# Attention with a gated MLP: V ahead of the third score tile at a unit's start, maxima transposed ahead of V, and 576 instead of 560 early score tiles that begin sooner

## The chip, the cores and the metric

The kernel runs on one core of a Trainium2 chip. The time is what the device takes for one execution, in microseconds (us), from start to end, with all loads from and stores to the chip's memory in it. "Before" is the kernel as it was, "after" the same kernel with the change below.

A core has five engines that run their own instruction streams and wait for one another by semaphores: TensorE (PE in the profile, its weight loads PEld), VectorE (DVE), ScalarE (ACT), GpSimd (POOL) and SyncE (SP). In this kernel SP only issues transfers, in the order of its queue.

## The reference

x has 2048 rows of 512. There are 32 heads of 16, and an MLP of width 1376 whose output gates the attention's.

```python
xn  = layernorm(x)
qkv = xn @ wqkv                                  # q, k, v: 32 heads x 2048 x 16
p   = softmax(q @ k.T * 16 ** -0.5)              # per head, 2048 x 2048
s   = (p @ v, heads joined) @ wo
g   = silu(gelu(xn @ w1 + b1) @ w2 + b2)
out = x + s * g
```

Everything is float32. The kernel splits most operands into a high and a low part and adds three products (`mm3`), and it keeps q and k as such pairs.

## The kernel before, in words

**Stages.** The first stage (to about 53 us) normalizes x, transposes it (`turn`), makes the q and k products of the first two head groups chunk by chunk (`q_first`), and four of the sixteen V products (`v_tile`). `evac` writes q and k, high and low, to scratch memory (`qk_h`, `qk_l`), from where they are loaded in the layout of attention: `load_k` for the keys of a group of four heads, `load_qs` for the queries of a *unit*. A unit is one group of heads times one chunk of 512 queries; there are 32 units.

The second stage (to about 480 us) is the written-out list `plan`: the other twelve V products (`quad`, entries "first"), the MLP's two products ("half" and "down") and the q and k products of the other groups. All its matmuls use half of the array's rows, two at a time, one on each half; `run` issues one for each half per *place*, counted in `prog["n"]`, 1488 places in all. After given places `run` calls hooks: splits and loads of weights, and `errand`, which takes one entry from the list `errands` (loads of K and Q for later units).

The third stage is attention, a loop of 512 steps (and one to drain): each step makes four transposed score tiles of 128 keys by 512 queries, one per head ("T", `t_one`), whose exponentials ScalarE writes (L656), and the V products of the step before ("V", `pv_step`, L723, a group of four heads, eight matmuls in the trace). From step 492 on the output products are woven in.

**The maxima.** The exponential needs each row's maximum before the T tiles of its unit start, so each score is made twice: once as an "S" tile of 128 queries by 512 keys (`s_one`, L174), whose maximum VectorE takes (L176), and later as a T tile. There are 2048 S tiles, 64 for each unit. An S tile uses one row half as well; `s_one` gets the half as its argument. 4 x `LEAD` = 560 of them are *early* tiles: `fill` puts them between the matmuls of the second stage, evenly from place `FILL0` on. The others go into the attention loop: `due(n)` says how many should exist at step n, and `ORDER` gives the order of a step's operations by the number of S tiles wanted. With three it is `STTTSTSV`, with four `STTSTSVTS`.

When a unit's S tiles are done, `s_end0` reduces the maxima and asks for the queries of the unit after the next. Some ticks later `flush` calls `s_end1` and `s_end2`: the maxima are transposed on TensorE (L200), copied out and written to memory (`mh_d`), from where `load_mh` brings them into the rows of QT that T multiplies.

**Banks.** S tiles take the accumulator banks of `s_ring` in turn. In attention that is twice the pool `ps_s`, which has two banks, and then the one of `ps_v` and `ps_x` that V does not use in this unit: V's sums for unit u are in `pv_pool(u)`, and at a unit's end ScalarE copies them out (`os`, L730). The transpose of the maxima takes a bank of the same ring.

**The code around the change.** In the attention loop, `tick` counts a waiting transpose down, and `flush` issues it, after a V group:

```python
            elif op == "V":
                if n:
                    pv_step(*divmod(n - 1, 16))
                for _ in range(4):
                    tick()
                flush()
```

Of the kernel before, what the change touches and what calls it, by code (L numbers as in the profile page):

```python
# [17 lines left out]
S = 2048  # L18
# [5 lines left out]
CH = 512  # L24
NCH = S // CH
# [4 lines left out]
EPS = 1e-5  # L30
SCALE = DH ** -0.5
VW = DH + 1
LEAD = 140
NW = 10
EARLY = 4
DONE = 492
FILL0 = 84
HB = 4
W2B = 2
ORDER = {0: "TTTTV", 1: "TTTTSV", 2: "TTTSTSV", 3: "STTTSTSV", 4: "STTSTSVTS"}  # L40
# [6 lines left out]
def fused(ctx: ExitStack, tc: tile.TileContext, x, wqk, wv, wo, w1, b1, w2, b2, out):  # L47
# [36 lines left out]
    NU = NG * NCH  # L84
# [14 lines left out]
    def load_k(g, pieces=range(6), eng=nc.sync, c0=0, n=S):  # L99
        both = kws[g % KB]  # L100
        for i in pieces:
            a, b = divmod(i, 3)
            r, cs = slice(64 * a + DH * b, 64 * a + DH * b + DH), slice(c0, c0 + n)
            src = rows((qk_h, qk_h, qk_l)[b], g, 1, a, c0, n)
            if both is not None:
                eng.dma_start(both[r, :, cs].bitcast(F32), src)
            else:
                for p in range(2):
                    eng.dma_start(kts[g % KB][p][r, cs].bitcast(F32), src[:, p])
# [23 lines left out]
    def load_qs(u, sides=range(2)):  # L133
        if u < NU:
            QS[u] = qzs[u % 2] if u < LEAD // 16 else qss[0][:, u % 2]
            q_rows(QS[u], u, sides)

    def ask_qs(u):
        for a in range(2):
            errands.append((load_qs, u, (a,)))  # L140
# [18 lines left out]
    def flush():  # L159
        while later and later[0][0] <= 0:  # L160
            u = later.pop(0)[1]
            s_end1(u)
            s_end2(u)

    def s_one(a):
        u, st, p = halves[a][made[a]]
        made[a] += 1
        g = u // NCH
        qi, ki = divmod(st, NCH)
        if u not in MX:  # L170
            MX[u] = qring.tile([P, GH, NCH, NCH], F32, name="mx")
        ps = s_tile()
        r, q = slice(64 * a, 64 * a + 3 * DH), QS[u]
        nc.tensor.matmul(ps, q[r, p, qi * P:(qi + 1) * P],  # L174
                         kts[g % KB][p][r, ki * CH:(ki + 1) * CH], start=True, stop=True)
        nc.vector.tensor_reduce(MX[u][:, 2 * p + a, qi, ki:ki + 1], ps, axis=AX.X, op=OP.max)  # L176
        if min(made) == 32 * (ended[0] + 1):
            v = ended[0]
            ended[0] += 1
            s_end0(v)  # L180
            later.append([12 if "seen" in prog else 8, v])
# [61 lines left out]
    for j in range(len(pairs)):  # L243
        for h in range(2):
# [4 lines left out]
            due = next((i for i in range(j, len(pairs)) if is_m[i]), len(pairs))  # L249
            nxt = next((i for i in range(j + h, len(pairs)) if is_m[i]), len(pairs))  # L250
            left = 2 * (nxt - j) + 1 - h
            need = 4 * sum(is_m[:nxt]) - 4 - nd
            room = 2 * (due + 1 - j) - h
            n = 2 if nd < len(parts) and parts[nd][2] and ready - nd > room else 1
            n = max(n, need - 2 * (left - 1))
# [27 lines left out]
    def w2_load(i):  # L283
        if i < len(ms):
            W2[ms[i][1:]] = w_new(w2[ms[i][2]], 2, "raw2")

    def w2_split(i):
        if i < len(ms):
            W2[ms[i][1:]] = w_split(W2[ms[i][1:]], "w2", W2B)
# [31 lines left out]
    with ExitStack() as s1:  # L321
# [54 lines left out]
        def v_tile(t):  # L376
            pv = a_tile((P, D))
            c, ts = t // NCH, slice(t % NCH * P, t % NCH * P + P)
            for k in range(KT):
                mm3(pv, (xh[c][:, k, ts], xl[c][:, k, ts]), (wv_h[:, k], wv_l[:, k]), k == 0, k == KT - 1)  # L380
            v_out(t, pv)

        def q_first(c):
            pq = {}
            for g in range(2):
                ps = pq["q", g, c] = a_tile((P, CH))
                for k in range(KT):
                    ks = slice(k * P, (k + 1) * P)
                    mm3(ps, (W1[g][0][:, ks], W1[g][1][:, ks]), (xh[c][:, k], xl[c][:, k]), k == 0, k == KT - 1)
            evac(list(pq), pq)  # L390
# [58 lines left out]
        for c in range(1, NCH):  # L449
            for t in range(NCH * c, NCH * c + NCH):  # L450
                turn(t)
            if c < NCH - 1:
                ln(NCH * c + NCH, NCH)
            else:
                nc.scalar.activation(warm[:, 1:], warm[:, :1], AF.Gelu_apprx_tanh)
                w1_load(0)
                w2_load(0)
                w2_load(1)
            v_tile(c - 1)
            q_first(c)  # L460
        v_tile(NCH - 1)

    keep_r = ctx.enter_context(tc.tile_pool(name="keep_r", bufs=1, side="right"))
    qring = ctx.enter_context(tc.tile_pool(name="qring", bufs=2, side="right"))
# [5 lines left out]
    qzp = qz.enter_context(tc.tile_pool(name="qzp", bufs=1, side="right"))  # L470
    for i in range(2):
        qzs.append(qzp.tile([P, 2, CH], F32R, name=f"qz{i}"))

    SYNC = mybir.DependencyInfo(mybir.DependencyClass.Sync, mybir.DependencyReason.DATA)
    prog.update(n=0, pe=0, seen=0)
# [141 lines left out]
    def quad(n):  # L617
        us = first[n]
        for u, b in zip(us, BANKS[n]):
            pool, name = {"x": (ps_x, "ps"), "m": (ps_m, "ps"), "v": (ps_v, "pv"), "t": (ps_t, "pst")}[b]  # L620
            PH[u] = pool.tile([P, CH], F32, name=name)
        for i in range(4):
            hooks = {6: [mark]} if i in (1, 2) else {}
            if n == VQ - 2 and i in (0, 2):
                hooks[3] = [lambda: w1_split(0) if i == 0 else w1_load(1)]
            run((terms(us[i], 0, i < 2), terms(us[(i + 2) % 4], 1, i < 2)), hooks)
            if i >= 2:
                for u in (us[i - 2], us[i]):
                    v_out(u[1] * NCH + u[2], PH.pop(u))
# [25 lines left out]
                         QT[u][r, p, :], start=True, stop=True)  # L655
        nc.scalar.activation(PT[u, k][:, 2 * p + a, :], ps, AF.Exp, scale=SCALE)  # L656

    load_k(0)
    load_qs(0)
    k_ones(kts[0])  # L660
    for n, e in enumerate(plan):
        if e[0] == "half":
            half(*e[1:])
        elif e[0] == "first":
            quad(e[1])
        else:
            if e[1] == parts[-2]:
                nc.scalar.activation(mhw, ident_r[:1, :1].bitcast(F32), AF.Exp)
            if e[1] == parts[-1]:
                for i in range(EARLY):  # L670
                    t_one(0, 0, i // 2, i % 2)
            down(*e[1])
        if e == ("first", VQ - 1):
            w2_split(0)
            w2_load(2)
            ask_qs(1)
            ask_k(1)
        if e[0] == "half" and pairs[e[1]][0] == ("q", NG - 1, 0) and e[2] == 1:
            kts.append([slot(p, (P, S), F32R) for p in range(2)])
            kws.append(None)  # L680
            qss.append(slot(2, (P, 2, 2, CH), F32R))
            ask_k(2)
        if n == len(plan) - 8:
            load_qt(0)
            load_mh(0)
# [151 lines left out]
    L = 16 * NU  # L837

    def due(n):
        return min(4 * L, 4 * LEAD + max(0, (4 * (L - LEAD) * n - 300) // (DONE - 1)))  # L840

    for u in range(NU):
        g, c = divmod(u, NCH)
        if c == 0 and g == KB:
            at(57, load_k, g, range(6), nc.gpsimd, 0, S // 2, pos=0)
            at(64, load_k, g, range(6), nc.gpsimd, S // 2, S // 2, pos=0)
        elif c == 0 and g > KB:
            for i in range(6):
                at(64 * (g - KB + 1) + 6 + i, load_k, g, (i,), nc.gpsimd, pos=0)
        if u >= 2:  # L850
            at(16 * u - 14, load_qt, u)
            need = min(n for n in range(L) if due(n) >= 64 * (u + 1)) + (4 if u < NU - 1 else 2)
            at(max(16 * u - 14, need), load_mh, u)
        if u < NU - 1:
            at(16 * u + 17, o_move, u, pos=0)
            at(16 * u + (25 if g < NG - 1 else 19), o_den, u, pos=0)
            at(16 * u + (31 if g < NG - 1 else 22), o_div, u, nc.gpsimd)
    T3 = range(NT - NCH, NT)
    last, late = 1, range(NW, NT)
    for t in range(NW):  # L860
        n = DONE + 2 * t
# [6 lines left out]
    for i, t in enumerate(late):  # L868
        n = L - 2 * len(late) - 1 + 2 * i
# [7 lines left out]
    for n in range(L + 1):  # L877
        ua, ka = divmod(n, 16)
        want = due(n) - sum(made)
        i = 0  # L880
        if n > 1 and (n - 1) % 16 == 0:
            s_ring[:] = [ps_s, ps_s, pv_pool((n - 1) // 16 + 1)]
            s_turn[0] = 0
        for op in ORDER[want] if n > 1 else ("TTTTV", "TTTVTSS")[n]:
            if op == "S":
                h = 1 - last if made[1 - last] - made[last] < 4 and made[1 - last] < 2 * L else last
                s_one(h)
                last = h
            elif op == "V":
                if n:  # L890
                    pv_step(*divmod(n - 1, 16))
                for _ in range(4):
                    tick()
                flush()
            else:
                if EARLY <= 4 * n + i < 4 * L:
                    t_one(ua, ka, i // 2, i % 2)
                    last = i % 2
                for f, args in todo.get((n, i), []):
                    f(*args)  # L900
                i += 1
# [56 lines left out]
```

## Time and profile before

| | |
|---|---|
| median of 3 runs | 1639.98 us (1639.7 to 1640.26) |
| the profiled execution | 1640.26 us, its span 1638.5 us |
| granted TensorE clock | 0.999 |
| PE busy | 1627.3 us (99%), 11656 matmuls |
| VectorE busy | 1389.8 us (85%) |
| ScalarE busy | 1271.9 us (78%) |
| GpSimd busy | 373.5 us (23%) |
| transfers | 116.83 MB, mean 71 GB/s |

The span goes from the first to the last instruction. Busy time is the time in which an engine had an instruction under way; matmuls overlap, so a busy PE is not PE at its peak. In a row of the timeline the first figure is the start in us from the span's start, the second the time it took (of merged rows, all of them), then engine, line, operation, what it writes and reads by the program's names, and the count; a bracket gives the idle time before it and what ended that. In a row of stretches the figures are: length, busy time (and instructions) of PE, PEld, DVE, ACT and POOL, then the granted clock, the mean busy share of the DMA engines and GB/s. In a row of waits: the engine and line that waited, for what, us in total, times, and for some the longest.

### The profile page before, as it was taken

Reading aid. Unit: us, or ns where it says so; the run is one execution under the profiler, and the core shown is the slowest. Engines: PE = TensorE matmul, PEld = TensorE weight load, DVE = VectorE, ACT = ScalarE, POOL = GpSimd, SP = SyncE. Lnnn points to the kernel's source line nnn. Section 1 sums busy time; section 2 is a strip of 40 time slices with the busy share of each in tenths; the row PEclk is TensorE's granted clock in tenths of the full one; section 3 lists DMA queues with packets and bytes.
Section 4 is the critical chain, followed back from the end, with each engine's and each line's share of the span. In section 5 each row is a group of like instructions: output and inputs, shape, how many; then the busy total and the mean of one; then the engine's idle time right before and its main releaser. Section 6 shows DMA issues by size and latency. Waiting matters only on the chain.

```text
span 1638.5 us, 31026 instructions
## 1 busy us (share of the span) xinstructions
PE 1627.3 (99%) x11656; PEld 898.3 (55%) x11656; DVE 1389.8 (85%) x2299; ACT 1271.9 (78%) x2523; POOL 373.5 (23%) x366
## 2 busy tenths in 40 slices
PE   9999999999999999999999999999999999999998
PEld 7898999988974434333334443433334443434445
DVE  7299999999988888888888888888888888888733
ACT  4333433434349999999999999999999999999984
POOL 4235565756630011001000100100100000000144
PEclk9999999999999999999999999999999999999999
DMA  6625334453330122112301411411141111110152
GB/s 200 147 72 150 113 118 130 138 135 121 111 117 26 29 50 47 31 45 49 61 26 28 79 29 28 66 31 31 36 59 32 28 28 37 32 28 22 56 191 94
DMA packets 76214, 116.83 MB, mean 71 GB/s; under 512 B 24964, under 2 KB 26244, under 8 KB 74696
## 3 DMA queue, kind: packets, MB, share of 16 engines
q1 hardware_dynamic: 72604, 102.42, 22.3%
q0 software_dynamic: 3264, 12.35, 4.5%
q8 instruction: 92, 1.51, 0.4%
q14 instruction: 58, 0.48, 0.1%
q10 hardware_dynamic: 196, 0.07, 0.0%
HBM read 84.35 MB, written 25.97 MB: 67 GB/s over the span
## 4 chain that ended last, share of the span: by engine, by line
PE 94%; DVE 2%; issue 2%; ACT 1%; POOL 1%; DMA 0%; SPq 0%; ACTq 0%; DVEq 0%; POOLq 0%
PE ps L174 23%; PE pv L723 15%; PE ps L723 15%; PE ps L506 12%; PE pst L654 12%; PE pst L506 7%; PE pv L174 3%; PE ps L77 2%; PE pv L506 2%; ACT slot L656 1%; PE pst L77 1%; POOL ol L791 1%; DVE mx L176 0%; PE ps L654 0%; POOL gx L824 0%
## 5 line engine op out<-in xcount | busy, mean ns | idle before, releaser
L176 DVE TENSOR_REDUCE mx<-ps 128x1 f32<-128x512 f32 x1808 | 1168.6, 685 | 160.3 <-PE ps L654 76.6
L656 ACT ACTIVATE slot<-pst 128x512 f32<-128x512 f32 x1533 | 806.9, 608 | 5.0 <-PE ps L174 4.5
L656 ACT ACTIVATE slot<-ps 128x512 f32<-128x512 f32 x515 | 308.7, 600 | 44.4 <-PE ps L654 9.8
L174 PE MATMUL ps<-kt,slot 48*128 48x512 f32 x864 | 327.9, 443 | 0.0
L174 PEld LDWEIGHTS ps<-kt,slot 48*128 48x128 f32 x864 | 158.2, 184 | 256.8 <-DVE mx L176 235.6
L654 PE MATMUL pst<-qt,kt 50*128 50x512 f32 x1149 | 294.1, 409 | 0.4 <-DVE gt L587 0.3
L723 PE MATMUL pv<-slot,vsb 128*32 128x512 f32 x2048 | 272.7, 605 | 0.0
L723 PE MATMUL ps<-slot,vsb 128*32 128x512 f32 x2048 | 272.5, 604 | 0.0
L506 PE MATMUL ps<-slot,w1h 64*128 64x512 f32 x1088 | 225.2, 394 | 0.4 <-ACT junk L519 0.4
L174 PE MATMUL ps<-kt,qz 48*128 48x512 f32 x512 | 211.1, 416 | 0.2
L654 PE MATMUL ps<-qt,kt 50*128 50x512 f32 x387 | 189.8, 492 | 0.0
L176 DVE TENSOR_REDUCE mx<-pv 128x1 f32<-128x512 f32 x240 | 163.8, 683 | 11.6 <-PE ps L654 7.8
L174 PE MATMUL ps<-slot,slot 48*128 48x512 f32 x432 | 166.2, 441 | 0.2
L506 PEld LDWEIGHTS ps<-slot,w1h 64*128 64x128 f32 x1088 | 153.8, 185 | 9.5 <-ACT junk L519 2.3
L654 PEld LDWEIGHTS pst<-qt,kt 50*128 50x128 f32 x1149 | 144.5, 186 | 21.5 <-issue 8.4
L506 PE MATMUL ps<-slot,w1l 64*128 64x512 f32 x544 | 154.0, 393 | 0.0
L174 PEld LDWEIGHTS ps<-slot,slot 48*128 48x128 f32 x432 | 78.6, 184 | 115.0 <-DVE mx L176 104.8
L307 POOL TENSOR_TENSOR hl<-hg,hh 128x512 fp32r<-128x512 f32 x76 | 96.9, 1297 | 129.2 <-ACT hh L306 80.8
L189 POOL TENSOR_TENSOR nmh<-nm,nmh 128x16 fp32r<-128x16 f32 x32 | 7.1, 221 | 497.9 <-DVE nm L188 266.5
L519 ACT ACTIVATE junk<-ident_r 1x1 f32<-1x1 f32 x91 | 17.8, 196 | 120.4 <-PE pst L506 104.0
L174 PEld LDWEIGHTS ps<-kt,qz 48*128 48x128 f32 x512 | 93.7, 183 | 11.8 <-DVE mx L176 2.7
L654 PE MATMUL pst<-qt,slot 50*128 50x512 f32 x384 | 97.7, 406 | 0.0
(161 smaller groups left out, 1980.7 us busy)
## 6 DMA issues: line engine op xcount, KB each, us to landing
raw<-in_w SPq DMA_DIRECT2D x88, 256.0 KB
qk_h<-hh SPq DMA_DIRECT2D x32, 256.0 KB
qk_l<-hl SPq DMA_DIRECT2D x32, 256.0 KB
qt<-qk_h SPq DMA_DIRECT2D x128, 64.0 KB
slot<-qk_h SPq DMA_DIRECT2D x96, 64.0 KB
xt<-in_x SPq DMA_DIRECT2D x16, 256.0 KB
g_d<-gt POOLq DMA_DIRECT2D x16, 256.0 KB, 3.7
qt<-qk_l SPq DMA_DIRECT2D x64, 64.0 KB
```

The costliest lines, as they stand in the source:

```text
L77: nc.tensor.matmul(ps, lhs[a], rhs[b], start=first and n == 0, stop=last and n == 2)
L174: nc.tensor.matmul(ps, q[r, p, qi * P:(qi + 1) * P], kts[g % KB][p][r, ki * CH:(ki + 1) * CH], start=True, stop=True)
L176: nc.vector.tensor_reduce(MX[u][:, 2 * p + a, qi, ki:ki + 1], ps, axis=AX.X, op=OP.max)
L189: nc.gpsimd.tensor_sub(NM[u][:, 1], nm, NM[u][:, 0].bitcast(F32))
L307: nc.gpsimd.tensor_sub(hl, raw, hh.bitcast(F32))
L506: i = nc.tensor.matmul(ps, lhs[r], rhs[r], start=first, stop=last).ins
L519: i = nc.scalar.activation(junk[:, :1], ident_r[:1, :1].bitcast(F32), AF.Copy).ins
L654: nc.tensor.matmul(ps, kts[g % KB][p][r, k * P:(k + 1) * P], QT[u][r, p, :], start=True, stop=True)
L656: nc.scalar.activation(PT[u, k][:, 2 * p + a, :], ps, AF.Exp, scale=SCALE)
L723: nc.tensor.matmul(PV[u][32 * j:32 * j + 32, :], vsb[:, k, h:h + 32], PT[u, k][:, j, :], start=(k == 0), stop=(k == NT - 1))
L791: lo.tensor_sub(ol[:, :n], src, oh[:, :n].bitcast(F32))
```

## The change

It does these things:

- `LEAD` is 144 instead of 140, so there are 576 early S tiles, and `due(n)` gives exactly three S tiles for each step from the second to step 491. Before, 1488 tiles were spread over the same steps, so that some had four.
- `FILL0` is 10 instead of 84: the early tiles begin at the start of the twelve V products. For that, the pools that hold K and Q are opened after the last transposes; three quarters of the first K and the first Q are loaded from there, ahead of the third V product and the last q and k products, and the last quarter of K after them. Unit 0 goes through its S tiles by chunks of keys first. Unit 1's queries are asked for after the first `quad` instead of after the third.
- In a unit's first step of attention the order `STTTSTSV` becomes `STTTSTVS`.
- `flush` comes before the V group instead of after it; a waiting transpose is still issued after the same number of ticks, and so lies ahead of the next step's V group instead of behind this step's.
- `load_mh` of the last unit moves by one step relative to the step in which its tiles are complete.

```diff
-LEAD = 140
+LEAD = 144
...
-FILL0 = 84
+FILL0 = 10
...
-        qi, ki = divmod(st, NCH)
+        qi, ki = divmod(st, NCH) if u else divmod(st, NCH)[::-1]
...
                 w2_load(1)
+                break
             v_tile(c - 1)
             q_first(c)
-        v_tile(NCH - 1)
...
+    load_k(0, c0=0, n=S - CH)
+    load_qs(0)
+    v_tile(NCH - 2)
+    q_first(NCH - 1)
+    v_tile(NCH - 1)
+    load_k(0, c0=S - CH, n=CH)
...
-    load_k(0)
-    load_qs(0)
     k_ones(kts[0])
...
             quad(e[1])
+            if e[1] == 0:
+                ask_qs(1)
...
         if e == ("first", VQ - 1):
             w2_split(0)
             w2_load(2)
-            ask_qs(1)
             ask_k(1)
...
     def due(n):
-        return min(4 * L, 4 * LEAD + max(0, (4 * (L - LEAD) * n - 300) // (DONE - 1)))
+        return min(4 * L, 4 * LEAD + max(0, 3 * n - 1))
...
-            need = min(n for n in range(L) if due(n) >= 64 * (u + 1)) + (4 if u < NU - 1 else 2)
+            need = min(n for n in range(L) if due(n) >= 64 * (u + 1)) + (4 if u < NU - 1 else 3)
...
-        for op in ORDER[want] if n > 1 else ("TTTTV", "TTTVTSS")[n]:
+        order = ORDER[want] if n > 1 else ("TTTTV", "TTTVTSS")[n]
+        if n > 1 and (n - 1) % 16 == 0 and order.endswith("SV"):
+            order = order[:-2] + "VS"
+        for op in order:
...
             elif op == "V":
+                flush()
                 if n:
                     pv_step(*divmod(n - 1, 16))
                 for _ in range(4):
                     tick()
-                flush()
```

## Prediction

> **What bounds the kernel now.** I read the page first: busy shares and the chain that ended last.
>
> ```profile
> PE 1627.3 (99%) x11656; PEld 898.3 (55%) x11656; DVE 1389.8 (85%) x2299; ACT 1271.9 (78%) x2523; POOL 373.5 (23%) x366
> ...
> PE 94%; DVE 2%; issue 2%; ACT 1%; POOL 1%; DMA 0%; SPq 0%; ACTq 0%; DVEq 0%; POOLq 0%
> ...
> L174 PEld LDWEIGHTS ps<-kt,qz 48*128 48x128 f32 x512 | 93.7, 183 | 11.8 <-DVE mx L176 2.7
> ```
>
> TensorE (PE) carries 94% of the chain. A busy PE can still be waiting, so next come the engines by stretches: one of the projections (first row) and the body of attention (second).
>
> ```profile
> 264.00:312.00 48.00, 48.00 (x396) 43.03 (x392) 44.21 (x69) 19.41 (x44) 31.93 (x28) 1.00 0.43 125
> ...
> 600.00:1520.00 920.00, 919.90 (x6402) 367.94 (x6396) 820.25 (x1373) 886.83 (x1725) 67.52 (x97) 1.00 0.19 39
> ```
>
> The busy figures stand in the order PE, weight loads, VectorE, ScalarE, GpSimd. In the projections VectorE (44.21 of 48 us) is at 92%, almost as tight as PE. In attention PE is full and ScalarE (886.83 of 920) close behind. What a change is worth there is read from the spacing of the V groups, so the third view is PE's timeline. A step runs from one V group (L723) to the next.
>
> ```profile
> 772.77 1.07 PE L723 MATMUL pv<-slot,vsb 128*32 128x512 f32 x8
> 773.76 0.25 PE L200 MATMUL ps<-ident_r,nmh 128*32 128x128 f32 x1
> 773.94 0.50 PE L174 MATMUL ps<-kt,slot 48*128 48x512 f32 x1
> ...
> 775.07 1.06 PE L723 MATMUL pv<-slot,vsb 128*32 128x512 f32 x8
> ...
> 794.12 1.06 PE L723 MATMUL pv<-slot,vsb 128*32 128x512 f32 x8
> ...
> 796.60 1.06 PE L723 MATMUL ps<-slot,vsb 128*32 128x512 f32 x8
> ...
> 798.72 1.07 PE L723 MATMUL ps<-slot,vsb 128*32 128x512 f32 x8
> 799.71 0.50 PE L174 MATMUL ps<-kt,slot 48*128 48x512 f32 x1
> ...
> 800.85 1.06 PE L723 MATMUL ps<-slot,vsb 128*32 128x512 f32 x8
> ...
> 807.22 1.07 PE L723 MATMUL ps<-slot,vsb 128*32 128x512 f32 x8
> ...
> 809.11 1.06 PE L723 MATMUL ps<-slot,vsb 128*32 128x512 f32 x8
> ...
> 810.10 0.72 PE L174 MATMUL ps<-kt,slot 48*128 48x512 f32 x2
> ...
> 811.41 0.50 PE L174 MATMUL ps<-kt,slot 48*128 48x512 f32 x1
> 811.84 1.06 PE L723 MATMUL ps<-slot,vsb 128*32 128x512 f32 x8
> ```
>
> Four kinds of step show. A plain one takes 2.13 us (798.72 to 800.85): 0.99 for V, then 1.14 for four T and three S tiles, which run two at a time on the two row halves. A step with a transpose of maxima (L200) takes 2.30. A unit's first step takes 2.48. A step of four S tiles and the next take 1.89 + 2.73 = 4.62, which is 0.37 over two plain ones (4.25).
>
> **The change, part by part.** *One S tile too many.* Before, 1488 score tiles are spread over 491 steps, so 15 steps carry a fourth; after, 1472 tiles make exactly three each. Saved: 15 x 0.37 = 5.6 us. Their 16 tiles move into the projections, where PE is also full: 24 products take 2.75 us there, 0.115 each.
>
> ```profile
> 67.31 2.75 PE pst L506 x24
> ```
>
> That costs 16 x 0.115 = 1.8 us. In exchange the early tiles thin out, from 560 over 1386 places to 576 over 1460 (2.4% less work for VectorE per place). The group of weight loads on the page's last row above waited 11.8 us in all, 2.7 of them for VectorE, so the gain lies between 0 and 2.7; I take 1.0.
>
> *First V ahead of the third S.* The 2.48 has its cause in two rows: ScalarE copies the old unit's sums out (os), and the third S needs that bank.
>
> ```profile
> 795.50 0.63 ACT L730 ACTIVATE os<-pv 128x512 f32<-128x512 f32 x1
> ```
>
> ```profile
> 796.18 0.18 PEld L174 LDWEIGHTS pv<-kt,slot 48*128 48x128 f32 x1 [0.31 <-ACT os L730]
> ```
>
> ```profile
> PEld pv L174 <- ACT os L730: 4.2, 14, 0.3
> PEld ps L174 <- ACT os L730: 4.2, 14, 0.3
> ```
>
> 28 of 30 boundaries show that wait. With V first it goes, and V's bank has long been free. But what is late next? The third S now opens the next step, and that step's own third S uses the same bank, three turns of the ring later. The four-S steps already have this order (`STTSTSVTS`): the S behind V starts at 810.10, VectorE reads it from 810.66, and the S that needs its bank starts only at 811.41, 1.31 later, with V 0.43 behind it.
>
> ```profile
> 810.66 1.29 DVE L176 TENSOR_REDUCE mx<-ps 128x1 f32<-128x512 f32 x2
> ```
>
> So I price a boundary as that pair: 1.89 + 2.73 = 4.62 against 2.48 + 2.12 = 4.60, or +0.02 each, +0.6 over 30. The 1.89 holds if the second S lies on the other row half than the fourth T; following the code's choice of halves step by step, it does at every boundary after the change. Ends: no wait for the bank (1.89 + 2.13) -0.58 each, -17; a fourth slot after all, +0.23 each, +7.
>
> *Maxima ahead of V.* The transpose now comes behind a step's third S and takes the ring's next bank, which is that of the step's first S: free 1.31 after that S started, where V would have started 1.14 after it. That is 0.17 of wait, and then V follows the transpose by up to 0.18 (773.76 to 773.94). Price 0.17 to 0.35, against 0.17 now (2.30 - 2.13). What queues behind the waiting transpose is the V group and with it everything on PE. Count:
>
> ```profile
> L208 DVE COPY mh<-ps x24: 268/274/279, 500.9 to 1555.7; 32x128 f32<-32x128 f32 x24
> ```
>
> 24 x (0 to 0.18) = 0 to 4.3; I take 0.1 each, +2.4. Nothing below zero, since the bank is always that one.
>
> *The early start.* The first S moves from place 87 to place 13 of the V products, which begin at 53.31 with 0.229 a place: it is due at 56.1. What it needs is K (six loads) and Q (six).
>
> ```profile
> 53.31 0.49 PE L506 MATMUL pst<-kt,slot 64*128 64x512 f32 x1
> ...
> 73.10 0.39 PE L174 MATMUL ps<-kt,qz 48*128 48x512 f32 x1
> ```
>
> ```profile
> 44.50 1.89 SPq L221 DMA_DIRECT2D raw<-in_w  x4
> ...
> 55.04 0.79 SPq L106 DMA_DIRECT2D kt<-qk_h  x2
> ...
> 65.58 0.30 SPq L131 DMA_DIRECT2D qz<-qk_h  x1
> ```
>
> ```profile
> 48.00:50.00 2.00, 2.00 (x11) 1.59 (x10) 0.00 (x0) 0.51 (x1) 0.00 (x0) 1.00 0.99 331
> 50.00:52.00 2.00, 2.00 (x10) 1.65 (x9) 0.00 (x0) 1.29 (x3) 0.04 (x1) 1.00 0.08 28
> ...
> 60.00:62.00 2.00, 2.00 (x20) 1.63 (x20) 0.00 (x0) 0.34 (x2) 0.00 (x0) 1.00 1.15 180
> ```
>
> On SP's queue the loads now follow the four weight loads of 44.50, so K can be asked for at 46.4 instead of 55.04; but the DMA engines work off those weights until 50. K's three quarters are 6 x 192 KB, Q's first half 0.2 MB: 1.38 MB at 180 GB/s (60:62, when K moved) is 7.7 us, plus about 2 to land: 59.5 to 60. Stall about 3.5 us. Ends: at the 331 GB/s of 48:50 hardly any; as long as before (55.04 to past 65.58) over 4. I take 3.4. All of PE waits behind that one S. The last K quarter is needed only at place 135, far behind its load.
>
> *Q of unit 2.* Unit 2 starts at place 337 instead of 404, but its Q is asked for by errands, one per half product. Moving unit 1's two errands up lets unit 2's run two turns earlier, at places 309 and 339; its second half is used at 340. Before, the errand of place 339 was the last K load. It went out at 147.46, and PE's S nearest place 340 started at 146.60.
>
> ```profile
> 146.60 0.39 PE L174 MATMUL ps<-kt,qz 48*128 48x512 f32 x1
> ```
>
> ```profile
> 147.46 0.43 SPq L106 DMA_DIRECT2D kt<-qk_l  x1
> ```
>
> ```profile
> SPq L755 <- DMA den_d<-dr: 78.0, 32, 10.2
> ```
>
> 0.86 late, two more issues of 0.43, and 78.0/32 = 2.4 for a small DMA to land: 4.1 us of PE waiting. Ends: 0, if SP runs ahead of PE there, and 4.5.
>
> *The clock.* Once in this trace PE falls idle that long, at its end:
>
> ```profile
> 1632.00:1635.00 3.00, 0.61 (x6) 0.41 (x4) 3.00 (x7) 0.00 (x0) 0.62 (x1) 0.93 0.47 175
> ```
>
> ```profile
> L420 PE MATMUL pv<-ident 128*128 128x128 f32 x23 | 5.2, 426 | 1.4 <-POOL ident masks.py:199 1.4
> ```
>
> ```profile
> L420 PE MATMUL pv<-ident 128*128 128x128 f32 x23 | 2.9, 285 | 0.0
> ```
>
> 0.93 means half clock from 2.6 us into that stretch, 2 us after PE's last work; two stalls of 3.4 and 4.1 should trip it too. The other two rows (0 to 6.4 us and 6.4 to 9) are the start: the same 23 transposes took 5.2 us and then 2.9, so about 5 us ran at half speed, 2.5 lost. Per stall 0 to 2.5; I take 2.0, together 4.0. The Trainium skill, "TensorE: Matmul & The Clock Gate", Part 1 (the HAM clock gate), says the gate is free-running: it halves the clock after an idle window of about 3.4 us and restores it after a busy one. The end of this trace agrees that idling halves it, though after only 2 us. By the page a stall would cost an estimated 1.7, and the sum would be 0.6 lower.
>
> Sum: -5.6 + 1.8 - 1.0 + 0.6 + 2.4 + 3.4 + 4.1 + 4.0 = +9.7 us. The profiled execution took 1640.26 (span 1638.5), 0.28 over the median of 1639.98; on the median that is 1649.7.
>
> **The rivals.** *The loads are in time.* K and Q land by 56 and SP issues unit 2's Q ahead of PE. Then 11.5 us fall away: 1638.2, not slower. It decides at a landing before 56.1 and an issue more than 3.3 us ahead of place 340. For it: 331 GB/s was reached just before. Against: K moved at 180, and unit 2's errand stands directly in front of its use. *One stall only*, with its clock: about 1643.9. *Both stalls without the clock loss*: 1645.7; for it, that no row shows a stall inside the run. *The boundary wait does not come*, its S finding its bank free: 17 to 18 less, 1631.6 with both stalls; against it the 1.31 above. *A fourth slot at each boundary*: +7, 1656.7.
>
> **How the numbers follow.** Forecast 0.45; no clock loss 0.17; one stall 0.15; loads in time 0.12; no boundary wait 0.06; fourth slot 0.05. About 0.2% (3.3 us) is what a measurement can tell from no change. Faster than that: the boundary case and the better part of the loads in time (its VectorE gain at 2.7, its transposes free), 0.09. Within: the rest of that and the small end of one stall, 0.13. Slower: 0.78. The range runs from 1638.0, which takes in half of the case without stalls, to 1654.5, where both stalls and the transposes stand at their upper ends; left out are the fourth slot, the free boundary and the other half, 0.17.
>
> **What would show it.** Right: first S between 59 and 61 with PE idle before it; a second idle stretch of about 4 us near 155, ended by a DMA of qz; PE's clock below 1.00 behind each; boundary pairs of 1.9 and 2.7; transpose steps of 2.3 to 2.5; no step of four S. Wrong: PE busy throughout 53 to 480, or boundary pairs summing to 4.1 or 4.8.

## The result, and the profile after

The changed kernel took **1656.74 us** (median of 4 runs, 1655.24 to 1657.85) against 1639.99 before, a ratio of 1.0102 with a 95% interval of 1.0084 to 1.0119: 16.75 us slower. The forecast was 1649.7. Its direction was right, its size was not, and the result lies 2.2 us above its range. The profiled execution took 1657.85 us, its span is 1656.1; between the two profiled spans lie 17.6 us.

The page of the changed kernel: engines, the chain that ended last, and the group of early score tiles (`qz`; the last two figures of a group are the idle time before it and what ended that).

```profile
PE 1631.1 (98%) x11656; PEld 903.3 (55%) x11656; DVE 1390.0 (84%) x2299; ACT 1268.7 (77%) x2525; POOL 372.1 (22%) x366
...
PE 95%; DMA 2%; DVE 2%; issue 0%; ACT 0%; POOL 0%; SPq 0%; DVEq 0%; ACTq 0%; POOLq 0%
...
L174 PE MATMUL ps<-kt,qz 48*128 48x512 f32 x512 | 209.4, 411 | 9.5 <-DMA qz<-qk_h 9.2
```

Transfers, 0% of the chain before, are now 2%, and 9.2 us of PE's idle time stand in front of the early tiles, ended by loads of queries. The rest must be found by stages. Their borders are PE's first half-row product (before, 53.31, shown in the prediction) and its first V group. Timeline of PE, first the kernel before, then after:

```profile
483.40 1.06 PE L723 MATMUL pv<-slot,vsb 128*32 128x512 f32 x8
```

```profile
55.74 0.50 PE L513 MATMUL pst<-kt,slot 64*128 64x512 f32 x1
...
498.83 1.07 PE L729 MATMUL pv<-slot,vsb 128*32 128x512 f32 x8
```

So the start lost 2.4 us (53.31 to 55.74) and the second stage 13.0 (430.09 to 443.09). From the first V to the end 2.2 are left; read in the same way, they are +0.4 in the first two steps, +3.1 in the loop up to step 490 and -1.3 behind it.

**The two stalls.** PE's timeline after, the last work ahead of each idle time and the tile that ended it:

```profile
58.37 0.39 PE L513 MATMUL pst<-kt,slot 64*128 64x512 f32 x1
64.00 0.76 PE L174 MATMUL ps<-kt,qz 48*128 48x512 f32 x1 [5.23 <-DMA qz<-qk_h]
...
160.74 0.39 PE L513 MATMUL ps<-slot,w1h 64*128 64x512 f32 x1
165.13 0.76 PE L174 MATMUL ps<-kt,qz 48*128 48x512 f32 x1 [3.99 <-DMA qz<-qk_h]
```

SP's queue around them (start, length, line, load):

```profile
46.96 1.91 SPq L221 DMA_DIRECT2D raw<-in_w  x4
49.06 0.80 SPq L106 DMA_DIRECT2D kt<-qk_h  x2
...
55.25 0.30 SPq L131 DMA_DIRECT2D qz<-qk_h  x1
57.39 0.30 SPq L131 DMA_DIRECT2D qz<-qk_l  x1
...
61.91 0.30 SPq L131 DMA_DIRECT2D qz<-qk_h  x1
...
161.27 0.38 SPq L131 DMA_DIRECT2D qz<-qk_h  x1
161.70 0.41 SPq L131 DMA_DIRECT2D qz<-qk_l  x1
162.16 0.41 SPq L131 DMA_DIRECT2D qz<-qk_h  x1
```

K and Q of the first unit were asked for behind the four weight loads, and the issues crept: the last of Q went out only at 61.91. The list of SP's own waits (49 to 64 us) says what held Q's loads (L131) back: SP waited until loads further ahead in its queue had landed, first the weights (`raw`), then K.

```profile
SPq L131 <- DMA raw<-in_w: 3.6, 2, 1.8
SPq L131 <- DMA kt<-qk_h: 2.3, 3, 1.0
```

Unit 2's Q went out at 161.27, when PE had just stopped (161.13), and PE went on 2.6 us behind the end of the last issue.

**The clock.** Stretches after (length; PE, PEld, DVE, ACT, POOL busy; granted clock; DMA share; GB/s):

```profile
62.50:69.30 6.80, 5.30 (x26) 4.55 (x28) 2.28 (x4) 0.20 (x1) 0.00 (x0) 0.50 0.82 227
69.30:72.00 2.70, 2.70 (x25) 2.38 (x22) 2.40 (x4) 0.00 (x0) 0.00 (x0) 1.00 0.06 21
164.90:168.30 3.40, 3.17 (x16) 2.75 (x18) 1.38 (x2) 0.00 (x0) 0.00 (x0) 0.50 0.00 0
168.30:171.00 2.70, 2.70 (x26) 2.43 (x23) 2.44 (x4) 0.56 (x3) 0.00 (x0) 1.00 0.03 6
```

Behind each stall the clock is 0.50. Half of PE's busy time there is lost: 5.30 / 2 = 2.65 us and 3.17 / 2 = 1.6 us. Stalls and clock make 5.2 + 4.0 + 2.65 + 1.6 = 13.5 of the second stage's 13.0.

**The start.** Two stretches, before and then after:

```profile
8.00:11.00 3.00, 2.32 (x21) 2.01 (x20) 2.64 (x9) 1.91 (x5) 0.00 (x0) 1.00 1.02 375
11.00:18.00 7.00, 5.66 (x26) 4.28 (x25) 6.55 (x14) 3.87 (x9) 6.59 (x8) 1.00 0.47 165
```

```profile
8.00:11.00 3.00, 0.70 (x7) 0.65 (x7) 2.52 (x10) 1.24 (x3) 0.00 (x0) 1.00 1.05 401
11.00:18.00 7.00, 6.31 (x21) 4.76 (x20) 6.60 (x15) 4.35 (x8) 6.21 (x6) 0.52 0.53 181
```

After, PE had 0.70 us of work from 8 to 11 where it had 2.32 before, and ran the next seven at a clock of 0.52. The code is the same there. Its warm-up products ended sooner (at 8.01 instead of 8.94) and its first transposes started later (10.31 instead of 9.62), so that PE stood idle for 2.30 us instead of 0.68. The four runs fall into two pairs, 1655.2 and 1655.9, 1657.6 and 1657.9, and their mean granted clocks go with that, 0.996 in both of the faster and 0.995 and 0.994 in the others. No other profile of this study shows the half clock there, so it is no part of the change that can be relied on.

**A unit's first step.** PE's timeline after, V groups, the last tiles of the first step and the two that share the disputed bank; then VectorE's reading of that bank:

```profile
811.02 1.06 PE L729 MATMUL pv<-slot,vsb 128*32 128x512 f32 x8
...
812.36 0.73 PE L661 MATMUL pst<-qt,slot 50*128 50x512 f32 x3
812.59 0.40 PE L174 MATMUL ps<-kt,slot 48*128 48x512 f32 x1
813.02 1.07 PE L729 MATMUL ps<-slot,vsb 128*32 128x512 f32 x8
814.02 0.50 PE L174 MATMUL pv<-kt,slot 48*128 48x512 f32 x1
...
815.30 0.50 PE L174 MATMUL pv<-kt,slot 48*128 48x512 f32 x1
815.73 1.07 PE L729 MATMUL ps<-slot,vsb 128*32 128x512 f32 x8
```

```profile
814.55 0.69 DVE L176 TENSOR_REDUCE mx<-pv 128x1 f32<-128x512 f32 x1 [0.71 <-PE pv L174]
```

The wait for ScalarE's `os` is gone from the list of waits. In its place the two tiles on the same bank (`pv`) start 1.28 apart, and the pair of steps takes 2.00 + 2.71 = 4.71; the median over 30 boundaries is 4.69.

**A transpose of maxima.** PE's timeline after, and the group's row:

```profile
828.57 1.06 PE L729 MATMUL ps<-slot,vsb 128*32 128x512 f32 x8
829.57 0.50 PE L174 MATMUL ps<-kt,slot 48*128 48x512 f32 x1
...
830.94 0.22 PE L200 MATMUL ps<-ident_r,nmh 128*32 128x128 f32 x1 [0.17 <-DVE mx L176]
831.09 1.07 PE L729 MATMUL ps<-slot,vsb 128*32 128x512 f32 x8
```

```profile
L200 PE MATMUL ps<-ident_r,nmh 128*32 128x128 f32 x32 | 7.3, 227 | 4.0 <-DVE mx L176 4.0
```

The step takes 2.52 where it took 2.30. The transpose waits about 0.17 for VectorE in 23 of 24 cases (4.0 us in all), and V follows it by 0.15. No step has four S tiles any more.

### The profile page after: what moved, and what is told of

Same layout as the page of the kernel before. It is cut to its first block, busy times and chain, and to the rows that moved or that the text cites. A ratio compares the mean times of both kernels' runs of the same rounds, so it can differ in the third digit from the quotient of the medians.

```text
span 1656.1 us, 31013 instructions
## 1 busy us (share of the span) xinstructions
PE 1631.1 (98%) x11656; PEld 903.3 (55%) x11656; DVE 1390.0 (84%) x2299; ACT 1268.7 (77%) x2525; POOL 372.1 (22%) x366
## 4 chain that ended last, share of the span: by engine, by line
PE 95%; DMA 2%; DVE 2%; issue 0%; ACT 0%; POOL 0%; SPq 0%; DVEq 0%; ACTq 0%; POOLq 0%
PE ps L174 23%; PE ps L729 15%; PE pv L729 15%; PE pst L661 12%; PE ps L513 12%; PE pst L513 7%; PE ps L77 3%; PE pv L174 3%; PE pv L513 2%; DVE mx L176 1%; PE ps L661 1%; PE pst L77 1%; DMA kt<-qk_h 1%; PE pv L77 1%; PE ps L200 0%
## 5 line engine op out<-in xcount | busy, mean ns | idle before, releaser
L174 PE MATMUL ps<-kt,slot 48*128 48x512 f32 x864 | 340.1, 449 | 0.5 <-DMA kt<-qk_l 0.5
L513 PE MATMUL ps<-slot,w1h 64*128 64x512 f32 x1088 | 221.5, 395 | 0.2 <-ACT junk L526 0.2
L661 PEld LDWEIGHTS pst<-qt,kt 50*128 50x128 f32 x1149 | 146.9, 186 | 20.6 <-ACT slot L663 12.3
L513 PEld LDWEIGHTS ps<-slot,w1h 64*128 64x128 f32 x1088 | 150.9, 186 | 11.1 <-ACT junk L526 2.9
L174 PE MATMUL ps<-slot,slot 48*128 48x512 f32 x368 | 146.0, 448 | 0.1
L513 PE MATMUL ps<-slot,w1l 64*128 64x512 f32 x544 | 145.1, 394 | 0.0
L174 PEld LDWEIGHTS ps<-slot,slot 48*128 48x128 f32 x368 | 66.7, 184 | 129.5 <-DVE mx L176 118.5
```

Source lines behind the costliest of these rows:

```text
L174: nc.tensor.matmul(ps, q[r, p, qi * P:(qi + 1) * P], kts[g % KB][p][r, ki * CH:(ki + 1) * CH], start=True, stop=True)
L513: i = nc.tensor.matmul(ps, lhs[r], rhs[r], start=first, stop=last).ins
L661: nc.tensor.matmul(ps, kts[g % KB][p][r, k * P:(k + 1) * P], QT[u][r, p, :], start=True, stop=True)
```

## The experiments

"The change" and eleven more kernels are in the table. "Stage 2" and "loop" are differences of the profiled execution from that of the kernel before, the stages as above (the loop from the third V to step 490). The ratio is against the kernel before, on the same chip, with its 95% interval.

| kernel | median us | ratio | stage 2 | loop |
|---|---|---|---|---|
| the change | 1656.74 | 1.0102 (1.0084 to 1.0119) | +13.0 | +3.1 |
| tiles_only | 1643.97 | 1.0025 (1.0015 to 1.0036) | +9.9 | -5.3 |
| v_first_only | 1644.86 | 1.0033 (1.0020 to 1.0045) | -0.1 | +5.0 |
| maxima_first_only | 1647.75 | 1.0050 (1.0037 to 1.0062) | +0.1 | +4.3 |
| early_only | 1647.66 | 1.0049 (1.0036 to 1.0061) | +8.6 | -0.3 |
| kq_ahead | 1653.32 | 1.0079 (1.0065 to 1.0092) | +11.5 | +3.1 |
| no_stalls | 1645.66 | 1.0034 (1.0021 to 1.0046) | +3.8 | +2.8 |
| best1 | 1638.04 | 0.9986 (0.9977 to 0.9995) | +4.4 | -5.2 |
| fewer_tiles | 1644.06 | 1.0022 (1.0013 to 1.0031) | -4.1 | +7.0 |
| vs_kept | 1641.77 | 1.0009 (1.0000 to 1.0017) | +4.0 | -1.4 |
| best2 | 1634.83 | 0.9967 (0.9955 to 0.9979) | +0.5 | -4.9 |
| best3 | 1655.13 | 1.0091 (1.0077 to 1.0105) | +0.3 | +15.8 |

The theory was the prediction's sum with sizes to be mended; the rivals were that other terms carried the loss, the tiles' price in the projections above all. The four kernels below the change in the table each put one part of it into the kernel before.

**tiles_only**: the 16 more early tiles, at the old places, and three S a step.

```diff
-LEAD = 140
+LEAD = 144
...
-        return min(4 * L, 4 * LEAD + max(0, (4 * (L - LEAD) * n - 300) // (DONE - 1)))
+        return min(4 * L, 4 * LEAD + max(0, 3 * n - 1))
```

> The kernel before with LEAD 144 and three S tiles in each step, nothing else. My theory (each part has its own price, and they add up): the 15 four-tile steps go, -5.6 us; the 16 tiles cost 1.8 us in the projections, VectorE's relief does not come here since the tiles lie denser (576 over 1386 places), and unit 2's queries, asked for 13 places ahead of their use, may cost up to 1 us: 1636 to 1638. Rival (the extra 0.37 of a four-tile step is work that only comes later): no gain, 1640 to 1642.

The loop gained 5.3 us, as the four-S steps had promised. But the 16 tiles cost 9.9 us in the second stage: 0.62 each, not the 0.115 of their matmul. Read with the next kernel.

**fewer_tiles**: the other way, 16 fewer early tiles in the kernel before.

```diff
-LEAD = 140
+LEAD = 136
```

> The kernel before with LEAD 136 in place of 140: 16 tiles fewer in the projections, 16 more steps of four in the loop. My theory (VectorE sets the pace of the projections, 0.62 us a tile): -9.9 there, +5.9 in the loop, 1635 to 1637. Rival (TensorE sets it, 0.115 a tile, and the 9.9 of the kernel with the tiles alone came from elsewhere): -1.8 and +5.9, 1643 to 1645.

A miss on the stage: it gained 4.1 us, 0.26 a tile, not 9.9. The loop lost 7.0, not 5.9. The time, 1644.06, lies in the rival's range, but the stage gained more than twice the rival's 1.8. The groups of the stretch 75 to 480 us show the early tiles' matmul (busy us, mean ns), in the kernel before, tiles_only and fewer_tiles:

```profile
L174 PE MATMUL ps<-kt,qz 48*128 48x512 f32 x509 | 209.9, 416 | 0.2
```

```profile
L174 PE MATMUL ps<-kt,qz 48*128 48x512 f32 x510 | 218.1, 430 | 0.3 <-ACT mh L206 0.3
```

```profile
L174 PE MATMUL ps<-kt,qz 48*128 48x512 f32 x510 | 206.3, 406 | 0.9 <-ACT mh L206 0.5
```

The denser the tiles, the longer each one. The same 360 us, in the kernel before and then in tiles_only (third busy figure: VectorE):

```profile
100.00:460.00 360.00, 359.75 (x2975) 325.86 (x2973) 332.46 (x515) 139.30 (x316) 218.21 (x187) 1.00 0.43 127
```

```profile
100.00:460.00 360.00, 359.71 (x2919) 327.68 (x2916) 331.00 (x517) 135.06 (x307) 215.29 (x184) 1.00 0.43 125
```

Tiles were planned 3% denser, yet VectorE did 517 instructions instead of 515, and PE 56 fewer. An estimate from the rows: with a place of 0.229 us and 0.115 for the tile, a tile comes every 1386 / 560 x 0.229 + 0.115 = 0.68 us before, every 0.67 with 576 and every 0.70 with 544. VectorE's reduction of one takes 0.69 (814.55 above). So by the estimate the kernel before sits at the knee: a tile more costs about VectorE's time (0.62), a tile less returns something between PE's and VectorE's. The list of waits hardly shows it: from 75 to 480 us it charges VectorE's reductions with 3.0 us in front of these tiles' weight loads in tiles_only, and with 3.5 in the kernel before. The lost time stands inside busy matmuls. Counted in the traces over the same stretch, 547 of 563 weight loads of early tiles in tiles_only began within 0.12 us, most often 0.05, after a VectorE instruction had ended (531 of 557 in the kernel before, 481 of 541 in fewer_tiles). A tile whose weights were loaded only as the tile itself began took 0.49 us (median), one whose weights lay ready 0.39, and the first kind grew with the density: 63 of 541 tiles in fewer_tiles, 110 of 557 in the kernel before, 210 of 563 in tiles_only. So VectorE holds PE back there; that a tile less returns 0.26 and a tile more costs 0.62 is not derived from it.

**v_first_only**: V ahead of the third S at a unit's start.

```diff
-        for op in ORDER[want] if n > 1 else ("TTTTV", "TTTVTSS")[n]:
+        order = ORDER[want] if n > 1 else ("TTTTV", "TTTVTSS")[n]
+        if n > 1 and (n - 1) % 16 == 0 and order.endswith("SV"):
+            order = order[:-2] + "VS"
+        for op in order:
```

> The kernel before with V ahead of the third S in a unit's first step, nothing else. My theory (the wait for the bank moves to the next step): the pair of steps takes 1.98 + 2.71 = 4.69 as in the profile after, against 4.60, +0.09 each over 30: 1642 to 1643. Where the second S lies on the same row half as the fourth T (here the choice of halves differs from the kernel after) the first step takes 2.13 and the pair 4.8. Rival (V first gains, and the loss in the profile after comes from the early part of the run): 0.3 to 0.6 less a boundary, 1622 to 1631.

The loop lost 5.0. Half of the boundaries came out as in the change (2.00 + 2.70), the other half at 2.12 + 2.71 = 4.83. With the old `due` the row halves of the tiles fall differently from unit to unit: in the shorter steps the second S and the fourth T start together, in the longer ones one after the other (692.88 and 693.11, with V at 693.43), which fits two tiles on the same half. For comparison, the 1.89 step that a four-S order makes in this kernel (808.73 to 810.62), and its last two weight loads:

```profile
810.29 0.39 PE L174 MATMUL pv<-kt,slot 48*128 48x512 f32 x1
810.30 0.39 PE L654 MATMUL pst<-qt,slot 50*128 50x512 f32 x1
810.62 1.06 PE L723 MATMUL ps<-slot,vsb 128*32 128x512 f32 x8
```

```profile
810.07 0.19 PEld L654 LDWEIGHTS pst<-qt,slot 50*128 50x128 f32 x1
810.08 0.18 PEld L174 LDWEIGHTS pv<-kt,slot 48*128 48x128 f32 x1
```

Here both tiles of the last pair had their weights 0.2 us ahead, took 0.39 each, and V started 0.32 after them. At a boundary of the changed kernel the last pair (812.59, above) is on the two halves as well, but the weights of its T were loaded only as it began:

```profile
812.59 0.18 PEld L661 LDWEIGHTS pst<-qt,slot 50*128 50x128 f32 x1
```

V started 0.43 after it. Counted over steps 3 to 489 of the kernel before, V followed a lone last tile by 0.32 (median of 418) where its weights lay ready, and by 0.43 (48) where they were loaded as it began. What the late load waits for was not tested.

**maxima_first_only**: the transposes ahead of V, with the last unit's load moved as in the change.

```diff
-            need = min(n for n in range(L) if due(n) >= 64 * (u + 1)) + (4 if u < NU - 1 else 2)
+            need = min(n for n in range(L) if due(n) >= 64 * (u + 1)) + (4 if u < NU - 1 else 3)
...
+                flush()
                 if n:
                     pv_step(*divmod(n - 1, 16))
                 for _ in range(4):
                     tick()
-                flush()
```

> The kernel before with the transpose of the maxima ahead of the V group, nothing else (the last unit's load of maxima one step later, as in the kernel after). My theory (the transpose waits for the bank of the step's first S and V waits with it): 24 transposes take 2.52 instead of 2.30, +5.3: 1644.5 to 1646. Rival (the longer transpose steps after the change come from the exact three tiles a step, not from the place): no change, 1640.

The loop lost 4.3, with transpose steps of 2.52 (2.30 before). Another 2.9 were lost at the end, where PE waits for the last unit's maxima:

```profile
1567.48 0.46 PE L654 MATMUL ps<-qt,kt 50*128 50x512 f32 x1 [1.15 <-DMA qt<-mh_d]
...
1568.32 0.71 PE L654 MATMUL pst<-qt,kt 50*128 50x512 f32 x3 [0.38 <-DMA qt<-mh_d]
```

and a clock of 0.50 for 3.4 us follows. In the whole change these tiles are done sooner and that wait does not come.

**early_only**: `FILL0` 10 with all the moved loads, 560 tiles.

```diff
-FILL0 = 84
+FILL0 = 10
...
+    load_k(0, c0=0, n=S - CH)
+    load_qs(0)
+    v_tile(NCH - 2)
+    q_first(NCH - 1)
+    v_tile(NCH - 1)
+    load_k(0, c0=S - CH, n=CH)
...
-    load_k(0)
-    load_qs(0)
...
+            if e[1] == 0:
+                ask_qs(1)
...
-            ask_qs(1)
```

> The kernel before with the early tiles from place 10 and all that goes with it (loads of K and Q sooner, keys by chunks, unit 1's errands sooner), with 560 tiles. My theory (PE waits for the first K and Q, then for unit 2's Q, and its clock halves behind each): 4.4 us and 3 us of half clock at the first S as in the profile after; unit 2's second half starts at place 347 instead of 340, 2 us later against its load, so that wait shrinks to about 2 and may not halve the clock; thinner tiles give back 1 to 2: 1646 to 1650. Rival (the stalls are given back because VectorE limits the projections): 1640 to 1642.

Both stalls are there without the other parts: PE was idle for 5.17 us from 56.7 and for 1.98 from 160.0, and the clock was 0.50 for 6.8 and 3.4 us behind them, with 4.7 and 3.4 us of work in it. Gaps and clock come to 5.17 + 1.98 + 2.4 + 1.7 = 11.2 us, the stage lost 8.6: some 2.6 came back, which is put down to the thinner tiles.

The four parts alone lose 4.3 + 5.1 + 8.0 + 8.0 = 25.4 us by their medians (1639.71 for the kernel before), the whole change 16.75. They do not add up, chiefly because the tiles' 9.9 are lost only at the old density: with 74 more places for them, VectorE has time.

The next kernels start from the changed one and take causes away.

**kq_ahead**: the weights (w1, w2) asked for behind K and Q.

```diff
-                w1_load(0)
-                w2_load(0)
-                w2_load(1)
                 break
...
     load_qs(0)
+    w1_load(0)
+    w2_load(0)
+    w2_load(1)
```

> The kernel after with the loads of the first K and Q issued ahead of the four weight loads that stood in front of them. My theory (the first stall is those 1 MB of weights): K and Q land 3 to 4 us sooner, PE's wait at the first S falls from 4.5 us to 1 or less, and its clock stays whole there, 3 us more: 1649 to 1653. Rival (the wait is K's own transfer time): 1656.

Only 3.4 us came back. Between the profiled executions 4.0 did, 1.5 of them in the second stage and 2.4 at the start, where this one has no half clock. The first wait shrank from 5.23 to 3.11, now for the low part of Q; the timeline, and the stretch at half clock:

```profile
59.44 0.76 PE L174 MATMUL ps<-kt,qz 48*128 48x512 f32 x1 [3.11 <-DMA qz<-qk_l]
```

```profile
58.60:65.40 6.80, 5.96 (x28) 5.20 (x30) 2.81 (x5) 0.20 (x1) 0.00 (x0) 0.50 1.06 307
```

SP's queue shows the pace of K's loads, for each of these issues waited for one of them to land:

```profile
52.83 0.30 SPq L131 DMA_DIRECT2D qz<-qk_l  x1
54.45 0.30 SPq L131 DMA_DIRECT2D qz<-qk_h  x1
```

They are 1.6 us apart with 192 KB a load; in the kernel before, with 256 KB, the same issues are as far apart (64.01, 65.58, 67.21). So the weights ahead of K were part of the delay and the number of K's loads the other. The second gap stayed (3.91 from 156.8).

**no_stalls**: also unit 2's Q ahead of K in the list of errands.

```diff
-            errands.append((load_qs, u, (a,)))
+            errands.insert(a if u == 2 else len(errands), (load_qs, u, (a,)))
```

> The same, and unit 2's queries asked for ahead of the K loads of unit 4. My theory (both stalls and the half clock behind them are 13.0 us of the 16.7): the second stretch takes about what it took before, the loop +3.1, 1642 to 1644. Rival (the 16 tiles cost VectorE's 0.62 each here too, as in the kernel with the tiles alone): 1651 to 1654.

Against the change, 11.1 us are back (1656.74 to 1645.66); between the profiled executions 12.2, of them 9.2 in the second stage and 2.7 at the start. The expected 1642 to 1644 was missed. The second gap is gone. The name promises too much: of the first, this is left in the list of waits (53 to 64 us), with one stretch of 3.4 us at half clock behind it.

```profile
PE ps L174 <- DMA qz<-qk_l: 2.5, 1, 2.5
```

**vs_kept**: no_stalls with the maxima behind V again. **best1**: with V's place at a unit's start undone as well.

```diff
-                flush()
                 if n:
                     pv_step(*divmod(n - 1, 16))
                 for _ in range(4):
                     tick()
+                flush()
```

> The kernel without stalls (no_stalls) with the maxima back behind V; V ahead of the third S stays. Its loop against that of best1 is the price of V first in the halves of the kernel after, and against no_stalls that of the maxima. My theory: 0.09 us a boundary, +2.7 over best1 in the loop, and the maxima the other 5: 1640.5 to 1641.5. Rival (the two parts have a price only together): as best1, 1638, or as no_stalls, 1645.7.

```diff
-        order = ORDER[want] if n > 1 else ("TTTTV", "TTTVTSS")[n]
-        if n > 1 and (n - 1) % 16 == 0 and order.endswith("SV"):
-            order = order[:-2] + "VS"
-        for op in order:
+        for op in ORDER[want] if n > 1 else ("TTTTV", "TTTVTSS")[n]:
```

> The same without stalls, and with the old places of V and of the maxima: what is left of the change is the early start and the 576 tiles. My theory: the loop is that of the kernel with the tiles alone (-5.3), the end too (-1.2), and the early start gives VectorE 74 more places, so that the 16 tiles cost nothing: 1633 to 1635. Rival (16 tiles cost 9.9 us wherever they begin): 1643.

The loops price both parts inside the change: maxima ahead of V +4.3 (2.8 against -1.4), V first +3.8 (-1.4 against -5.2). With neither, three S a step are worth 5.2, as in tiles_only. By pairs of steps V first costs only 2.5. The other 1.3 lie in the seven units in which a transpose of maxima stands two steps behind the boundary: in best1 it is in the first of these steps (2.30), in vs_kept in the second (2.30), and the first mostly takes 2.25 even so. best1 missed its 1633 to 1635, with 4.4 lost in the second stage: a wait of 2.73 for Q was left, and 3.4 us at half clock behind it.

**best2**: best1 with the early tiles from place 32.

```diff
-FILL0 = 10
+FILL0 = 32
```

> best1 with the early tiles from place 32 in place of 10, so that the first S comes at 60 us, behind the landing of Q. My theory (what was left of the first stall, 2.5 us and 1.7 of half clock, goes; 22 places fewer for VectorE cost back 1 to 2): 1634 to 1636. Rival (an idle PE there is free, since VectorE sets the pace to the end of the projections): 1638 to 1640.

The first S comes at 61.28, after its loads. PE waits for none, and the clock stays at 1.00 through the second stage, which is within 0.5 us of the kernel before although it carries 16 tiles more. At 1634.83 us it is faster than both kernels.

**best3**: best2 with V ahead of the third S in every step.

```diff
-ORDER = {0: "TTTTV", 1: "TTTTSV", 2: "TTTSTSV", 3: "STTTSTSV", 4: "STTSTSVTS"}
+ORDER = {0: "TTTTV", 1: "TTTTSV", 2: "TTTSTSV", 3: "STTTSTVS", 4: "STTSTSVTS"}
```

> best2 with V ahead of the third S in every step, not only in a unit's first. My theory (the bank's wait of 1.3 us comes from two third tiles in one step's span; if all lie behind V, they are a whole step apart, and only at a unit's end V waits about 0.15 for its bank): a boundary of 2.3 in place of 2.48, 4 to 6 us less than best2: 1628 to 1632. Rival (a third tile next to the next step's first costs a place on TensorE each step): 1638 or more.

The loop lost 20.7 us against best2. The reason that it should gain fell: 23 of the 30 boundary pairs took 4.83 in place of 4.60, since a tile ahead of V waits there for VectorE to free its bank:

```profile
801.36 0.50 PE L174 MATMUL ps<-kt,slot 48*128 48x512 f32 x1 [0.32 <-DVE mx L176]
```

That is 5.5 of the 20.7. About half of the other steps took 2.18 instead of 2.13; in 126 steps of best3 the last tiles ahead of V are a pair with weights loaded as it begins, which V follows by 0.38 (median) instead of 0.32, but the 2.18 was not followed further.

## Why the prediction was wrong in size

**Right: both stalls and the clock.** The second stage was forecast at 1.8 - 1.0 + 3.4 + 4.1 + 4.0 = +12.3 and lost 13.0. That the sum came so close is partly luck: the first stall was 1.8 longer, and the tiles cost 0.8 less than forecast. *The early start* took 5.23 instead of 3.4. The working had the cause (K and Q land too late for the first S), but the step "1.38 MB at 180 GB/s" failed. K went out as assumed, 6.7 us ahead of PE's first half-row product instead of 6.9; 2.4 of the 2.7 us between 46.4 and 49.06 are the start. But a load of K takes 1.6 us whether it has 192 or 256 KB, so that six take 9.6 where their bytes at 180 GB/s give 6.6, and the weights, which the working had off the DMA engines by 50, held back Q's issues until 57.39. So the first S came at 64.00 and not between 59 and 61. *Q of unit 2* was 3.99 against 4.1, by the mechanism given: the errand stood directly in front of its use.

*The clock* was 2.65 + 1.6 = 4.2 against 4.0. kq_ahead and no_stalls took the two causes away one after the other, the first of them in part, and 9.2 of the stage's 13.0 came back. (The rows of L420 that the working calls transposes are the kernel's warm-up products; that changes nothing in the sum.) The Trainium skill, "TensorE: Matmul & The Clock Gate", Part 1 (the HAM clock gate), gives the window as about 3.4 us and the throttled state as half: the stretches of 3.4 and 6.8 us at 0.50 agree, one window and two. The Trainium skill's window is an idle one, and one such window gave the estimate of 1.7 a stall. The measurement differs in that the window need not be wholly idle: in early_only PE stood idle for only 1.98 us (160.04 to 162.01) and the clock fell. The second stall cost about the estimate (1.6). Behind the first the clock stayed at half for a second window, after one in which PE had worked for only 1.9 us (64.0 to 65.9), as if that were too little to restore it; how much a window needs, no run here measured.

**Wrong by cancellation: one S tile too many, its price in the projections.** The step that failed is "24 products take 2.75 us there, 0.115 each": it priced a tile by PE, although VectorE's 92% stood one paragraph above. tiles_only measured 0.62. In the sum it did little harm, by luck, since the same change gives the tiles 74 more places: stalls and clock alone make 13.5 of the 13.0, so all 16 tiles came for about nothing, where +0.8 was forecast. best2 shows it without stalls: +0.5. The loop's gain of 5.6 was right (5.3).

**Wrong in size: maxima ahead of V.** The mechanism was right (the bank is that of the step's first S), the size was not. The step that failed is "I take 0.1 each"; it should have been the upper end, 0.18, and a little more: V cannot start under the transpose (it follows by 0.15), and the bank comes free 1.37 after the first S, not 1.31. Measured 0.22 each, in the 22 transpose steps of the loop; the loop lost 4.3, not 2.4.

**Wrong in size: first V ahead of the third S.** The bank's 1.31 was right (1.28), and so was the second step (2.71 for 2.73). The step that failed is the 1.89 of the first, taken from four-S steps: it is 1.97 to 2.00. Its condition held, the second S lies on the other half than the fourth T at every boundary, but the weights of one of the two are loaded only as it begins, and V follows 0.40 to 0.43 behind instead of 0.32. So a boundary is 4.69, not 4.62. By pairs that is about +2.5 over 30, by the loops of vs_kept and best1 +3.8; +0.6 was forecast.

**Not foreseen.** The early clock loss is 2.4 us of the profiled execution; that the two faster runs are without it is argued from their clocks and times, since they have no profile. Even they lie above 1654.5. The end of the kernel gave 1.3 back, in every kernel with three S a step where the last maxima come in time; why was not tested.

Mended, the sum is 2.4 (start) + 13.0 (stage 2) + 0.4 - 5.3 + 3.8 + 4.3 - 1.3 = 17.3, against 17.6 between the spans. Of the 7.9 us by which the forecast of 9.7 fell short of that, 2.4 are the start, 5.1 the two orders in attention, and the rest small. The rival that came nearest in time, the fourth slot (1656.7), was not what happened: no boundary took 4.83 in the changed kernel.

## What to carry to other kernels

A tile that is added to a stage costs the time of whichever engine handles it slowest: where two engines are both above 90%, price it by each, and expect the price of one more and of one less to differ. When work is pulled ahead of its loads, the wait costs its own length and then the clock; begin it where its data has landed (here 22 places later), and look at what stands in front of its load in the issuing queue. Parts of a change that move an operation by a fraction of a step should be tried one by one: here one of the four was worth 5 us, two cost 4 each, and the fourth was right only with another number and with two loads moved.

## What the runs showed of the hardware

- The granted clock fell to 0.50 for 6.8 us behind waits of 5.23, 5.17 and 3.11 us, and for 3.4 us behind waits of 3.99, 3.91, 2.73, 2.5 and 1.98. Within the runs, nothing between 3.4 and 6.8 was seen. A longer wait does not always cost more: in the kernel after, 5.30 us of work fell into the first stretch, in kq_ahead, with the shorter wait, 5.96.
- PE need not be wholly idle: at the start of the profiled execution after, 0.70 us of work in three was followed by seven at 0.52. In tiles_only 1.18 us of work in the same three were not.
- Loads of K, each into few partitions, landed 1.6 us apart, with 192 KB (kq_ahead) as with 256 KB (the kernel before).
- A tile of 512 columns whose weights lay ready took 0.39 us, one whose weights were loaded as it began 0.49 to 0.50. A V group started 0.32 us after the start of the first kind (810.30 to 810.62 in v_first_only), and 0.40 to 0.43 after that of the second (815.30 to 815.73), whether the tile was alone or one of a pair.
